# A recurrent segment loop on one core: output projection in four column quarters, the last tokens projected at the end

## The chip, the cores and the metric

The kernel runs on one core of one Trainium2 chip, with TensorE (matmul), VectorE, ScalarE, GpSimd, SyncE and the core's 16 DMA engines. The metric is the device time of one execution in microseconds, as a median of runs; a profiled execution of the same kernel gives the page and the trace that are read here.

## What is computed

Two independent parts write the two halves of the columns of one output, 2048 x 2048 in bf16. Part A is a long convolution (`_A_ref`), which the change leaves alone. Part B is a transformer layer with a memory that is passed from segment to segment:

```python
mem = mem0                                    # [1, 8, 1024]
for s in range(64):                           # 64 segments of 32 tokens
    h = concatenate([mem, x[:, 32*s:32*s+32]])          # 40 rows of 1024
    q, k, v = (einsum('btd,dhe->bhte', h, W) for W in (Wq, Wk, Wv))   # 32 heads of 128
    p = softmax(where(mask, einsum('bhqe,bhke->bhqk', q, k) * scale, -1e9))
    o = einsum('bhte,hed->btd', einsum('bhqk,bhke->bhqe', p, v), Wo)  # 40 rows of 1024
    mem = o[:, :8]                            # next segment's memory
    outs.append(o[:, 8:])                     # this segment's 32 tokens
```

The memory rows of one segment's output are input rows of the next, so the segments run one after the other.

## The kernel before

Part A runs first, with the parts of B that need no memory beside it: K, Q and V of the last 8 tokens of every segment, which are stored in the DRAM tensors RKQ (K and Q) and VBD (V). Then the loop over 64 segments runs from an order written out by hand (`tc.manual_schedule`): every engine executes its instructions in the order of the source, and semaphores make it wait. Each segment handles 32 rows on TensorE, 8 of memory and the first 24 tokens; the last 8 tokens join as keys, values and queries from RKQ and VBD.

**Weights.** The four matrices are cut in 64 pieces of 512 KB (128 x 2048 bf16): 16 each of Wk, Wq and Wv by rows (`kc`) and column half (`g`), and 16 head pairs (`hp`) of Wo. Most stay in SBUF under the names Wres, Wmid, Wmore, Wlate, pw, Wring and whole. The positions in STREAM of the list ORDER are streamed instead: `fetch` (L736) loads them from a DRAM copy WS into a ring of five slots (`wring`), on SP's queue, and `done` (L911) frees a slot after a piece's last matmul and fetches the next. Two of the streamed pieces of Wo (KEPT_A, pair 13, and KEPT_B, pair 9) are read once and kept as four quarters each in unused columns of PSUM; from segment 1 on VectorE copies a quarter to SBUF (`quarter` L893, `quarter_b` L856, through `bits`, L851) before its matmuls. 13 pieces are left to load in each segment.

**A segment.** `Proj.run` (L980) multiplies the 32 rows by a piece of Wk, Wq or Wv in four groups of 32 columns of the array, 512 columns each, into a PSUM bank; `evac` (L993, L989) copies the bank to SBUF on ScalarE. `transposes` turns K and Q (L935, L1002), `scores` (L1008, L1011) multiplies them in PSUM, `softmax_a` and `softmax_b` (L1015, L1025) run on VectorE with one exponential on ScalarE, and `attend` (L1052, L1056) multiplies by V. All this happens for two halves of 16 heads (g = 0 and 1). In the scores' block of eight groups of 40 columns, groups 0 to 3 belong to the 32 rows, one for each of four heads, and groups 4 to 7 to the last 8 tokens, for which one of the four groups is the right one for a row (`rowhead`).

**The output projection.** `evac_o` (L1064) copies the attention output OT of 16 heads to SBUF, 40 columns a head. `project` (L1074) takes 64 of these columns as weights (24 are of the next head and not used) and multiplies one head by 256 columns of Wo, in two groups of 64 columns of the array (`dh`), which hold the two halves of the 1024 output columns; `f` chooses 256 of the 512 in a half, in PSUM bank `yacc[f]`. So f = 0 and f = 1 are two passes. The order is: pairs 0 to 5, then `attend(1)`, pairs 6 and 7 while OT1 leaves PSUM, then the heads of g = 1 with the kept quarters laid between them, at last the five pairs of LAST for f = 0 and for f = 1. Each `yacc[f]` goes to the SBUF tile Y (L1170), and `fill_mem` (L778) turns the memory rows of Y into the next segment's input hT by matmuls with an identity and a copy on VectorE (L780). Two DMAs on GpSimd's queue store 32 rows of 512 columns each (L1172).

**GpSimd's queue in a segment, in order:** `load_kq` of the next segment (L930) within the projection, the two output stores, `keys(0)` (L964, a copy that needs `load_kq`), two VBD loads (L959), `keys(1)`, and `load_x` of the next segment (L769), which waits until V's matmuls have read the one buffer `rec`.

**SBUF rooms.** A tile `arena` of 21 blocks of 128 columns holds the segment's small data; `room(name, n)` is n blocks from a named start: C 0, D 4, B 8, KT1 12, A 13, KQ 17.

Of the kernel before, what the change touches and what calls it, by code (L numbers as in the profile page):

```python
# [9 lines left out]
BF = mybir.dt.bfloat16  # L10
# [11 lines left out]
FIRST, LAST = (0, 1, 2, 3), (10, 15, 11, 12, 14)  # L22
KEPT_A, KEPT_B = (3, 13, 0), (3, 9, 0)
WHOLE = (3, 4, 0)
O_ORDER = (*FIRST, 4, 5, 6, 7, 9, 13, 8, *LAST)
ORDER = [(0, kc, 0) for kc in (0, 1, 4, 5)] + [(1, kc, 0) for kc in (0, 1)] + [(0, kc, 0) for kc in (2, 3, 6, 7)] + \
    [(1, kc, 0) for kc in range(2, 8)] + [(m, kc, 1) for m in (0, 1) for kc in range(8)] + \
# [407 lines left out]
def b_kernel(ctx: ExitStack, tc, x, mem0, Wq, Wk, Wv, Wo, outb, n_seg, run_a):  # L435
    nc = tc.nc
# [41 lines left out]
    RKQ = dram.tile([n_seg // 16, 4, 128, 16, 128], BF, name="RKQ")  # L478
    VBD = dram.tile([2, n_seg, 8, 16, 128], BF, name="VBD")
# [41 lines left out]
    def stage1_done(su, vl, spare):  # L521
        make_consts()
        pools["mid"] = ctx.enter_context(tc.tile_pool(name="b_wmid", bufs=1, reuse_waits="tile"))
        for i, ch in enumerate(parts[0]):
            res[ch] = pools["mid"].tile([128, 2048], BF, name=f"Wmid{i}")[:]
# [246 lines left out]
    mem_cols = ident[:].rearrange("p (dh x) -> p dh x", dh=2)[:, :, 0:NM]  # L772

    def fill_mem(hT, Y, half, wide=32, tp=None):
        tp = tps[:, 0, 0:128].bitcast(F32) if tp is None else tp
        for j in (2 * half, 2 * half + 1):
            for e in range(0, 128, wide):
                nc.tensor.matmul(tp[e:e + wide, 16 * j:16 * j + 16], lhsT=Y[:, j * 128 + e:j * 128 + e + wide], rhs=mem_cols,  # L778
                                 start=True, stop=True, skip_group_check=True, tile_position=(0, e))
        nc.vector.tensor_copy(  # L780
            hT.rearrange("p (dh j) t -> p dh j t", dh=2)[:, :, 2 * half:2 * half + 2, 0:NM],
            tp.rearrange("p (j dh r) -> p dh j r", j=4, dh=2)[:, :, 2 * half:2 * half + 2, :])

    with c0p:
# [17 lines left out]
        Y = room("D", 4)  # L802
        nc.vector.memset(Y, 0.0)
        with tc.issue_after(got[-1].ins):
            load_x(0)
            for dh in range(2):
                nc.gpsimd.dma_start(Y[64 * dh:64 * dh + NM, :], mem0[:, dh * 512:(dh + 1) * 512])
        for g in range(2):
# [3 lines left out]
            for tb in range(4):  # L812
                if g == 1 and tb == 3:
                    for half in range(2):
                        fill_mem(pend[0], Y, half, tp=ps0.tile([128, 64], F32, tag="ps0", name="mem_ps")[:])
# [40 lines left out]
    def quarter_b(q, tag):  # L856
        t = room(tag, 4).bitcast(I32)
        w = []
        for home, at in B_homes[q]:
            n = home.shape[1] * (home.shape[2] if len(home.shape) == 3 else 1)  # L860
            bits(like(t[:, at:at + n], home), home)
            part = room(tag, 4)[:, 2 * at:2 * at + 2 * n]
            for dh, o in enumerate(quarter_cols(q)):
                lo, hi = max(at, 128 * dh), min(at + n, 128 * dh + 128)
                if lo < hi:
                    w.append((o + 2 * lo - 256 * dh, o + 2 * hi - 256 * dh, part[:, 2 * (lo - at):2 * (hi - at)]))
        return w

    def quarter_cols(q):
        return [1024 * (q // 2) + 512 * dh + 256 * (q % 2) for dh in range(2)]  # L870

    def keep(ch):
        t = live[0, ch][1]
        if kept[ch] == "A":
            w = t[:].bitcast(I32).rearrange("p (hh dh f x) -> p hh f dh x", hh=2, dh=2, f=2)
            for q in range(4):
                bits(OTi[:, q, 160:416].rearrange("p (dh x) -> p dh x", dh=2), w[:, q // 2, q % 2])
        else:
            w = t[:].bitcast(I32)
            for q in range(4):  # L880
                for home, at in B_homes[q]:
                    n = home.shape[1] * (home.shape[2] if len(home.shape) == 3 else 1)
                    if len(home.shape) == 3 and n > 128:
                        for dh, o in enumerate(quarter_cols(q)):
                            bits(home[:, 2 * dh:2 * dh + 2, :], w[:, o // 2:o // 2 + 128].rearrange("p (b x) -> p b x", b=2))
                        continue
                    for dh, o in enumerate(quarter_cols(q)):
                        lo, hi = max(at, 128 * dh), min(at + n, 128 * dh + 128)
                        if lo < hi:
                            src = w[:, o // 2 + lo - 128 * dh:o // 2 + hi - 128 * dh]  # L890
                            bits(home if len(home.shape) == 3 else home[:, lo - at:hi - at], like(src, home))

    def quarter(q, tag):  # L893
        t = room(tag, 4)
        bits(t.bitcast(I32), OTi[:, q, 160:416])
        return [(o, o + 256, t[:, 256 * dh:256 * dh + 256]) for dh, o in enumerate(quarter_cols(q))]
# [41 lines left out]
    with tc.manual_schedule():  # L938
# [6 lines left out]

        def seed_scores():
# [5 lines left out]
        for s in range(n_seg):  # L952
# [62 lines left out]
            def softmax_a(tag):  # L1015
                mx = one.tile([128, 8], F32, tag="mx", name="mx")
                nc.vector.tensor_reduce(out=mx[:], in_=S, op=ALU.max, axis=AX.X)  # L1017
                E = room(tag, 5).bitcast(F32).rearrange("p (b k) -> p b k", b=8)
                nc.vector.tensor_tensor(out=E, in0=S, in1=mx[:].unsqueeze(2).to_broadcast([128, 8, 40]),  # L1019
                                        op=ALU.subtract)  # L1020
                seed_scores()
                nc.scalar.activation(E, E, ACT.Exp, scale=scale)  # L1022
                return E

            def softmax_b(E, tag):  # L1025
                ssum = one.tile([128, 8], F32, tag="mx", name="ssum")
                nc.vector.tensor_reduce(out=ssum[:], in_=E, op=ALU.add, axis=AX.X)
                nc.vector.reciprocal(ssum[:], ssum[:])
                nc.vector.tensor_tensor(out=ssum[:, 4:8], in0=ssum[:, 4:8], in1=rowhead[:], op=ALU.mult)
                nc.vector.tensor_tensor(out=P_pad[:, 0:4, 0:32], in0=E[:, 0:4, 0:32],  # L1030
                                        in1=ssum[:, 0:4].unsqueeze(2).to_broadcast([128, 4, 32]), op=ALU.mult)
                own = P_pad[:].rearrange("p b k -> p (b k)")[:, 32:320].rearrange("p (i w) -> p i w", w=72)
                nc.vector.tensor_tensor(out=own[:, 0:4, 0:8], in0=E[:, 0:4, 32:40],
                                        in1=ssum[:, 0:4].unsqueeze(2).to_broadcast([128, 4, 8]), op=ALU.mult)
                nc.vector.tensor_tensor(out=E[:, 4:8, :], in0=E[:, 4:8, :],
                                        in1=ssum[:, 4:8].unsqueeze(2).to_broadcast([128, 4, 40]), op=ALU.mult)
                nc.vector.tensor_copy(P_pad[:, 4, 32:64].rearrange("p (i t) -> p i t", i=4), E[:, 4:8, 32:40])
                with nc.allow_low_precision("one of the four terms is not zero"):
                    nc.vector.tensor_reduce(out=P_pad[:, 4, 0:32], in_=E[:, 4:8, 0:32].rearrange("p i k -> p k i"),
                                            op=ALU.add, axis=AX.X)  # L1040
                PT = room(tag, 3)[:, 0:320].rearrange("p (kb i q) -> p kb i q", kb=2, i=4)
                for kb in range(2):
                    ks = slice(32 * kb, 32 * kb + 32)
                    nc.vector.transpose(out=PT[:, kb, :, 0:32], in_=P_pad[:, 0:4, ks])
                    nc.vector.transpose(out=PT[:, kb, :, 32:40], in_=P_pad[:, 4, ks])
                return PT

            def attend(g, PT, V):
                for i in range(4):
                    w = V[i // 2][:, i % 2 * 128:i % 2 * 128 + 128]  # L1050
                    for c in range(4):
                        nc.tensor.matmul(OTp[:, c, i * 40:i * 40 + 40], lhsT=w[32 * c:32 * c + 32, :],  # L1052
                                         rhs=PT[32 * c:32 * c + 32, 0, i, :], start=(i == 0), stop=False,
                                         tile_position=(32 * c, 0), skip_group_check=True)
                for c in range(4):
                    nc.tensor.matmul(OTp[:, c, 0:160], lhsT=VBs[g][32 * c:32 * c + 32, :],  # L1056
                                     rhs=PT[32 * c:32 * c + 32, 1].rearrange("p i q -> p (i q)"), start=False, stop=True,
# [4 lines left out]
            def evac_o(g):  # L1062
                OT = room("B" if g else "C", 5).rearrange("p (c i q) -> p c i q", c=4, i=4)
                nc.scalar.copy(OT, o_view)  # L1064
                return OT

            def project(h, f, w, OT, stop=False):
                k = 40 * (h % 16)
                m = min(64, 640 - k)
                lhsT = OT.rearrange("p c i q -> p (c i q)")[:, k:k + m]  # L1070
                for dh in range(2):
                    o = (h % 2) * 1024 + dh * 512 + f * 256
                    for x, y, r in columns(w, o, o + 256):
# [171 lines left out]
```

## Time and profile before

| what | time or size |
|---|---|
| runs | 1716.27, 1721.94, 1723.39 us (median 1721.94) |
| profiled execution, own time | 1717.88 us |
| its span on the core | 1716.0 us |
| part A and setup, to the first output projection | 398 us |
| TensorE busy | 1644.0 us (96%) |
| VectorE, ScalarE, GpSimd busy | 1033.6, 675.9, 348.8 us |
| moved by DMA | 598.03 MB, mean 348 GB/s |
| TensorE clock granted in the loop | full |

A page has the busy time of each engine, the span in 40 slices, the DMA queues, the chain of work that ended last, and the costliest groups of instructions. Matmuls are pipelined: a single one lasts 379 ns, but a new one can start long before, so the rate is read from how many matmuls fill a stretch, not from the length of one.

### The profile page before, as it was taken

Reading aid. Unit: us, or ns where it says so; the run is one execution under the profiler, and the core shown is the slowest. Engines: PE = TensorE matmul, PEld = TensorE weight load, DVE = VectorE, ACT = ScalarE, POOL = GpSimd, SP = SyncE. Lnnn points to the kernel's source line nnn. Section 1 sums busy time; section 2 is a strip of 40 time slices with the busy share of each in tenths; the row PEclk is TensorE's granted clock in tenths of the full one; section 3 lists DMA queues with packets and bytes.
Section 4 is the critical chain, followed back from the end, with each engine's and each line's share of the span. In section 5 each row is a group of like instructions: output and inputs, shape, how many; then the busy total and the mean of one; then the engine's idle time right before and its main releaser. Section 6 shows DMA issues by size and latency. Waiting matters only on the chain. (4 is left out here: it accounts for less than half of the span.)

```text
span 1716.0 us, 71162 instructions
## 1 busy us (share of the span) xinstructions
PE 1644.0 (96%) x30776; PEld 996.9 (58%) x30776; DVE 1033.6 (60%) x3463; ACT 675.9 (39%) x1250; POOL 348.8 (20%) x626
## 2 busy tenths in 40 slices
PE   6899988998999999999999999999999999999998
PEld 3443333445666666666666666666666666666665
DVE  9968853235555555656666555555565656655555
ACT  6876741103333333333333333333333333333333
POOL 4113431101122111211211212121121112111121
PEclk9999998999999999999999999999999999999999
DMA  9989999989999999999999999999999999999997
GB/s 330 391 310 378 373 346 372 357 321 374 344 346 341 346 350 348 360 342 353 352 353 354 341 354 344 340 357 352 347 350 347 352 333 355 356 345 342 349 354 277
DMA packets 180830, 598.03 MB, mean 348 GB/s; under 512 B 24658, under 2 KB 24674, under 8 KB 180516
## 3 DMA queue, kind: packets, MB, share of 16 engines
q1 hardware_dynamic: 151860, 525.80, 84.4%
q0 software_dynamic: 19984, 44.61, 7.4%
q10 hardware_dynamic: 8672, 23.07, 3.4%
q8 instruction: 241, 3.95, 0.9%
q14 instruction: 73, 0.60, 0.1%
HBM read 538.33 MB, written 57.15 MB: 347 GB/s over the span
## 5 line engine op out<-in xcount | busy, mean ns | idle before, releaser
L980 PEld LDWEIGHTS <-rec 128*32 128x32 bf16 x12288 | 298.4, 96 | 284.0 <-DVE rec L780 36.3
L1074 PEld LDWEIGHTS <-arena 128*64 128x64 bf16 x8255 | 430.0, 109 | 51.6 <-ACT arena L1064 33.4
L993 ACT CAST arena<-acc 128x512 bf16<-128x512 f32 x320 | 187.0, 584 | 359.7 <-PE acc L980 288.0
L980 PE MATMUL acc<-Wres,rec 128*32 128x512 bf16 x3328 | 251.0, 381 | 3.2 <-issue 3.2
L980 PE MATMUL acc<-wring,rec 128*32 128x512 bf16 x2300 | 227.5, 380 | 4.4 <-issue 1.6
L980 PE MATMUL acc<-Wmid,rec 128*32 128x512 bf16 x3072 | 211.7, 379 | 0.3 <-issue 0.2
L1074 PE MATMUL yacc<-Wmore,arena 128*64 128x256 bf16 (+1 forms) x2560 | 207.6, 273 | 0.2 <-issue 0.2
L1064 ACT CAST arena<-OTp 128x640 bf16<-128x640 f32 x128 | 88.6, 692 | 197.6 <-PE OTp L1056 177.0
L1104 DVE COPY arena<-OTp 128x512 bf16<-128x512 bf16 x64 | 27.2, 425 | 230.3 <-PE OTp L935 230.3
L1074 PE MATMUL yacc<-wring,arena 128*64 128x256 bf16 x2064 | 159.8, 274 | 3.5 <-DMA wring<-WS 1.8
L851 DVE TENSOR_SCALAR arena<-OTp 128x256 int32<-128x256 int32 x378 | 128.0, 394 | 38.0 <-ACT arena L1064 35.2
L1074 PE MATMUL yacc<-arena 128*64 128x256 bf16 x1071 | 141.1, 270 | 0.1
L1170 ACT CAST arena<-yacc 128x256 bf16<-128x256 f32 x128 | 47.7, 373 | 230.2 <-PE yacc L1074 226.7
L980 PE MATMUL acc<-pw,rec 128*32 128x512 bf16 x1796 | 121.8, 379 | 2.1 <-issue 1.4
L959 POOL DMA_DIRECT2D arena<-VBD x128 | 68.3, 534 | 259.7 <-DVE arena L1019 104.6
L980 PE MATMUL acc<-Wlate,rec 128*32 128x512 bf16 x1536 | 117.0, 381 | 0.0
L780 DVE CAST rec<-tps 128x32 bf16<-128x32 f32 x126 | 24.2, 192 | 148.8 <-PE tps L778 148.8
L1172 POOL DMA_DIRECT2D out_dram<-arena x128 | 65.8, 514 | 203.7 <-ACT arena L1170 200.4
L930 POOL DMA_DIRECT2D arena<-RKQ x64 | 49.6, 775 | 253.5 <-PE yacc L1074 244.4
L1017 DVE TENSOR_REDUCE mx<-SB 128x8 f32<-128x320 f32 x128 | 62.7, 490 | 47.0 <-PE SB L1011 43.6
L1022 ACT ACTIVATE arena<-arena 128x320 f32<-128x320 f32 x128 | 60.3, 471 | 69.0 <-DVE arena L1019 60.5
L769 POOL DMA_DIRECT2D rec<-REC x64 | 35.9, 561 | 247.9 <-PE acc L980 244.2
(225 smaller groups left out, 2633.5 us busy)
## 6 DMA issues: line engine op xcount, KB each, us to landing
wring<-WS SPq DMA_DIRECT2D x831, 512.0 KB, 5.9
SK<-s_sb SPq DMA_DIRECT2D x16, 512.0 KB, 7.6
SU<-s_sb SPq DMA_DIRECT2D x16, 512.0 KB, 6.7
Kg<-SK SPq DMA_DIRECT2D x32, 256.0 KB, 5.8
Ug<-SU SPq DMA_DIRECT2D x32, 256.0 KB, 5.5
RKQ<-stage ACTq DMA_DIRECT2D x16, 512.0 KB, 9.6
zt<-SZ SPq DMA_DIRECT2D x16, 512.0 KB, 10.6
arena<-RKQ POOLq DMA_DIRECT2D x64, 128.0 KB, 5.7
```

The lines of the kernel that those rows point to most:

```text
L769: nc.gpsimd.dma_start(rec[:], REC[:, s, :])
L851: nc.vector.tensor_scalar(out=dst, in0=src, scalar1=0, scalar2=None, op0=ALU.bitwise_or)
L930: nc.gpsimd.dma_start(rec.rearrange("p (j c) -> p j c", j=4), RKQ[s // 16, :, :, s % 16, :].rearrange("j p c -> p j c"))
L959: nc.gpsimd.dma_start(VB, VBD[g, s].rearrange("t h e -> h t e"))
L980: nc.tensor.matmul(self.acc[32 * c:32 * c + 32, :], lhsT=hT[:, ch[1], :], rhs=w[:, 512 * c:512 * c + 512], start=(ch == chs[0]), stop=(ch ...
L993: nc.scalar.copy(sb, self.acc[:])
L1017: nc.vector.tensor_reduce(out=mx[:], in_=S, op=ALU.max, axis=AX.X)
L1022: nc.scalar.activation(E, E, ACT.Exp, scale=scale)
L1064: nc.scalar.copy(OT, o_view)
L1074: nc.tensor.matmul(yacc[f][64 * dh:64 * dh + m, x - o:y - o], lhsT=lhsT, rhs=r, start=(h == (0, 2 * FIRST[-1])[f] and x == o), stop=stop, ...
L1170: nc.scalar.copy(Y[:, 256 * f:256 * f + 256], yacc[f][:, 0:256])
L1172: nc.gpsimd.dma_start(bass.AP(outb.tensor, outb.offset + SEG * s * 2048 + 512 * dh, [[2048, 32], [1, 512]]), Y[64 * dh + NM:64 * dh + 40, :])
```

## The change

- Each head's projection takes exactly its 32 columns of OT as weights, in four groups of 32 columns of the array at once, each for a quarter of the 1024 output columns (`head_out`). One PSUM bank `Yb` holds all 256 columns of the four quarters, so pairs 0 to 9 need one pass of 256 columns, and LAST two passes of 128.
- The last 8 tokens of each segment are no longer projected in the loop. `evac_last` copies their columns of OT and stores them on GpSimd's queue in a DRAM tensor OLD (two stores of 32 KB a segment, rows of 256 bytes). After the loop they are loaded in four blocks of 16 segments (`last_rows`), put in order by head (`by_heads`) and multiplied as 128 rows by all of Wo; the six streamed pieces of Wo are loaded again for it (`ends`).
- Output in the loop is 24 rows in four stores of 256 columns.
- The right group of scores for the last 8 tokens is selected (a multiply and a sum) ahead of the softmax, which then works on five groups instead of eight; two transposes replace four.
- All eight pairs of g = 0 (EARLY) come ahead of `attend(1)`. Kept quarters come in another order, two of them (B0 and A2) copied on ScalarE; `load_kq` follows quarter A2.
- PSUM banks of the projections alternate with the segment's parity; the copy of Q after its first transposition moves to ScalarE; the order of `kc` within K and Q changes with the layout of the memory rows. The streamed positions stay the same.

```diff
+EARLY, LAST = (0, 1, 2, 3, 4, 5, 6, 7), (10, 15, 11, 12, 14)
+O_ORDER = (*EARLY, 9, 13, 8, *LAST)
+ORDER = [(0, kc, 0) for kc in (0, 2, 4, 6)] + [(1, kc, 0) for kc in (0, 2)] + [(0, kc, 0) for kc in (1, 3, 5, 7)] + \
+    [(1, kc, 0) for kc in (4, 6, 1, 3, 5, 7)] + [(m, kc, 1) for m in (0, 1) for kc in range(8)] + \
...
+        def last_rows(b):
+            for g in range(2):
+                raw[b, g] = home(6 + 2 * b + g, "OLr")
+                nc.sync.dma_start(raw[b, g][:].rearrange("p (s w) -> p s w", s=16), OLD[:, g, 16 * b:16 * b + 16, :])
+        def by_heads(b, engines):
+            for g in range(2):
+                OLs[b, g] = home(2 * b + g if b < 3 else 14 + g, "OL")
+                engines[g](
+                    OLs[b, g][:].rearrange("p (h s t) -> p h s t", h=16, s=16),
+                    raw[b, g][:].rearrange("p (s h t) -> p h s t", s=16, h=16))
...
-                    self.acc = bank(g if m == 2 else m, "acc")
+                    self.acc = bank((g if m == 2 else m) ^ s % 2, "acc")
...
+                nc.vector.tensor_tensor(out=own, in0=S[:, 4:8, :], in1=rowhead[:].unsqueeze(2).to_broadcast([128, 4, 40]),
+                                        op=ALU.mult)
+                nc.vector.tensor_reduce(out=S[:, 4, :], in_=own.rearrange("p i k -> p k i"), op=ALU.add, axis=AX.X)
+                nc.vector.tensor_reduce(out=mx, in_=S[:, 0:5, :], op=ALU.max, axis=AX.X)
...
-                nc.scalar.copy(OT, o_view)
+                main = OT[:, 0:512].rearrange("p (c i q) -> p c i q", c=4, i=4)
+                for c in range(0, 4, 2 if g else 4):
+                    cs = slice(c, c + (2 if g else 4))
+                    nc.scalar.copy(main[:, cs], o_view[:, cs, :, 0:32])
+            def evac_last(g, OT):
+                nc.scalar.copy(OT[:, 512:640].rearrange("p (c i q) -> p c i q", c=4, i=4), o_view[:, :, :, 32:40])
+                nc.gpsimd.dma_start(OLD[:, g, s, :], OT[:, 512:640])
+            def head_out(h, lo, hi, OT, rhs_of, stop=False):
+                for qd in range(4):
+                    nc.tensor.matmul(Yb[32 * qd:32 * qd + 32, lo:hi], lhsT=OT[:, 32 * (h % 16):32 * (h % 16) + 32],
+                                     rhs=rhs_of(qd), start=(h == 0), stop=stop, skip_group_check=True,
+                                     tile_position=(0, 32 * qd))
...
             V1 = pv1.evac()
+            evac_last(0, OT0)
+            if last:
+                for b in range(3):
+                    last_rows(b)
+                for i, hp in enumerate(hp for hp in O_ORDER if (3, hp, 0) in streamed):
+                    ends[hp] = home(16 + i, "Wend")[:]
+                    nc.sync.dma_start(dst_view(ends[hp], (3, hp, 0)), dram_chunk((3, hp, 0)))
+                by_heads(0, [nc.gpsimd.tensor_copy] * 2)
+            Yb = bank(s % 2, "yacc")
+            for hp in EARLY:
+                out_cols(hp, 0, 256, OT0)
+            qs = {}
+            if s:
+                qs["B", 0] = quarter_b(0, "KQ", by_act)
             attend(1, PT1, (V1[:, 0:256], V1[:, 256:512]))
             OT1 = evac_o(1)
+            if s:
+                qs["A", 0], qs["B", 2] = quarter(0, "C", bits), quarter_b(2, "A", bits)
+                out_quarter(KEPT_B, 0, qs["B", 0])
+                qs["A", 2] = quarter(2, "KQ", by_act)
+                steps = {(0, 0): [("A", 0), ("B", 1, "C", bits)], (0, 2): [("B", 2), ("B", 3, "A", bits)], (0, 3): [("A", 2)],
+                         (1, 1): [("B", 1), ("A", 1, "C", bits)], (1, 2): [("B", 3), ("A", 3, "A", bits)],
+                         (1, 4): [("A", 1), ("A", 3)]}
...
+            evac_last(1, OT1)
+            out_cols(8, 0, 256, OT1)
...
+                            if step == ("A", 2) and not last:
+                                load_kq(s + 1)
...
+            for q in range(4):
+                nc.gpsimd.dma_start(bass.AP(outb.tensor, outb.offset + SEG * s * 2048 + 256 * q, [[2048, NX], [1, 256]]),
+                                    Y[32 * q + NM:32 * q + 32, :])
+            if last:
+                last_rows(3)
+        for b in range(4):
+            if b < 3:
+                by_heads(b + 1, [nc.vector.tensor_copy, nc.scalar.copy])
             for dh in range(2):
+                z = bank(dh, "z")
+                for h in range(32):
+                    o = 1024 * (h % 2) + 512 * dh
+                    nc.tensor.matmul(z[:], lhsT=OLs[b, h // 16][:, 128 * (h % 16):128 * (h % 16) + 128],
+                                     rhs=ends.get(h // 2, res.get((3, h // 2, 0)))[:, o:o + 512], start=h == 0, stop=h == 31)
+                zs = room("C" if dh else "B", 4)
+                (nc.vector.tensor_copy if dh else nc.scalar.copy)(zs, z[:])
+                nc.sync.dma_start(bass.AP(outb.tensor, outb.offset + (512 * b + NX) * 2048 + 512 * dh,
+                                          [[SEG * 2048, 16], [2048, 8], [1, 512]]), zs)
```

`out_cols(hp, lo, hi, ...)` calls `head_out` for the two heads of a pair, and `out_quarter` for one kept quarter.

More of the change, by code (lines that the diff above doesn't have):

```diff
@@ L1062, in evac_o @@
             def evac_o(g):
-                OT = room("B" if g else "C", 5).rearrange("p (c i q) -> p c i q", c=4, i=4)
-                nc.scalar.copy(OT, o_view)
-                return OT
[L1067 to L1073, printed above, removed]
-                        nc.tensor.matmul(yacc[f][64 * dh:64 * dh + m, x - o:y - o], lhsT=lhsT,
-                                         rhs=r, start=(h == (0, 2 * FIRST[-1])[f] and x == o), stop=stop,
-                                         tile_position=(0, 64 * dh))
```

210 lines of the change are left out of this document (88 added, 122 removed).

## The prediction

> **What bounds the kernel now.** I read the page's slices and queues first, then the chain of waits for one segment, then the timeline of the same stretch of another, then windows for the transfers.
>
> ```profile
> PE   6899988998999999999999999999999999999998
> DMA  9989999989999999999999999999999999999997
> q1 hardware_dynamic: 151860, 525.80, 84.4%
> wring<-WS SPq DMA_DIRECT2D x831, 512.0 KB, 5.9
> ```
>
> TensorE and the 16 DMA engines are both full from the tenth slice on. Nearly all that moves is the weight ring (`wring`): 13 pieces of 512 KB in each of the 64 segments.
>
> ```profile
> 1332.19 2.74 PE yacc L1074 x48
> 1334.93 0.20 PE OTp L1052 x16
> 1335.13 0.07 PE OTp L1056 x4
> 1335.21 4.14 PE yacc L1074 x72
> 1339.35 0.06 PE tps L778 x2
> 1339.41 0.46 PE yacc L1074 x8
> 1339.87 0.98 PE acc L980 x16
> 1340.85 0.04 PE tps L778 x7
> 1340.88 3.32 PE acc L980 x60
> 1344.20 0.45 PE OTp L935 x32
> ...
> 1352.31 2.74 PE yacc L1074 x48
> ```
>
> In the chain, one segment is TensorE alone and takes 20.12 us from one output projection to the next: 7.68 us of projection (1332.19 to 1339.87), then 12.44 us of K, Q, V and attention. From 1270.14 to 1703.87 the same row comes 21 times later, so the mean segment is 433.73/21 = 20.65 us; the 0.53 us over 20.12 are scattered gaps. From the start of the first projection (398.36 in the timeline) to that of the last (1703.80) lie 63 segments, and 12.2 us from there to the end.
>
> ```profile
> 285.00:305.00 20.00, 17.30 (x85) 8.02 (x84) 8.26 (x9) 3.52 (x6) 1.99 (x3) 0.91 1.03 419
> 1001.00:1006.00 5.00, 5.00 (x106) 4.42 (x103) 3.94 (x18) 1.43 (x3) 0.56 (x1) 1.00 1.00 371
> 1006.00:1011.00 5.00, 5.00 (x104) 3.64 (x104) 1.84 (x8) 0.75 (x2) 1.80 (x3) 1.00 0.93 317
> 1011.00:1016.00 5.00, 5.00 (x140) 2.69 (x132) 1.72 (x4) 1.76 (x3) 1.04 (x3) 1.00 1.01 364
> ```
>
> The last two columns are the DMA engines' share and GB/s. Within the loop a share of 1.00 goes with about 370 GB/s: of the forty 5 us windows from 500 to 700 us, the 17 with a share of 1.00 or more have a mean of 372 and reach from 347 to 390. From 500 to 1700 us the mean is 349 GB/s, so a segment moves 349 x 20.65 = 7.21 MB. The DMA engines are thus hardly looser than TensorE, though TensorE rarely waits for `wring` by name: the five ring slots are refilled 5.9 us ahead.
>
> **What the change removes on TensorE.** Rates come from the chain. Four 32-column groups at 512 columns: 3.32/15 = 0.221 us for four (L980). At 128 columns: 0.45/8 = 0.056 us for four (L935). Two 64-column groups at 256 columns: 0.114 us for two (L1074). Four at 256 columns appear nowhere; half of 0.221 and the whole of 0.114 bound them at 0.110 and 0.114, and I take 0.112. After: heads of EARLY 16 x 0.112 = 1.8; pair 8, 0.22; eight quarters of kept weights, 0.45; LAST, 20 x 0.056 = 1.1. That is 3.6 us of matmul where 7.4 stood.
>
> **What gives most of it back.** The old matmuls were cover. Let S be the start of the projection.
>
> ```profile
> 1019.46 0.49 DVE L1017 TENSOR_REDUCE mx<-SB 128x8 f32<-128x320 f32 x1
> 1021.31 0.49 DVE L1027 TENSOR_REDUCE ssum<-arena 128x8 f32<-128x320 f32 x1
> 1023.70 0.17 DVE L1045 STREAM_TRANSPOSE arena<-P_pad 128x32 bf16<-128x32 bf16 x1
> 1023.98 0.17 PEld L1052 LDWEIGHTS <-arena 32*128 32x128 bf16 x16 [0.20 <-issue]
> ```
>
> Here S = 1021.24. The second softmax starts on VectorE at S-1.78 and lets `attend(1)` go at S+2.74. The new one puts a multiply (L1035's size, 0.34) and a reduction (L1039's, 0.37) ahead; maximum and subtraction shrink from 0.49 to about 0.37 (320 elements to 200). With the 0.14 us between dependent operations the sum starts at S+0.85 instead of S+0.07. Behind it, fewer operations take 2.1 us for 2.6. So `attend(1)` goes at about S+3.05, while EARLY is done at S+1.8: 1.25 us idle. Then 0.28 for `attend(1)`; then OT1 must leave PSUM (two ScalarE halves of L989's 0.375, plus 0.3 of semaphores) before any OT1 head can start: 0.65 idle, which pairs 6 and 7 used to cover. From S+4.0 there are 1.8 us of matmuls, laid between kept quarters copied out of PSUM at 0.36 to 0.59 us each into three rooms in turn; I count waits of 0.1 (A2), 0.3 (B3), 0.35 (A3) and 0.15 for `fill_mem`. Sum: S+6.7, against S+7.68. The other side of the same step: `load_x` issues at S+0.49 and lands 5.2 later in the middle (4.3 to 6.5), and the next K needs it and a 0.19 copy, so S+6.1 is the floor and S+7.4 the bad case. I take 6.7. Bank alternation and QT0 on ScalarE get nothing: TensorE is busy in `k1.run(5)` while QT0 is copied, and the next K starts with no wait for the accumulators' banks in the chain above. TensorE's segment: 12.44 + 6.7 + 0.53 = 19.65 us.
>
> **The transfers.** Ring loads stay 13. Added per segment: two stores of 32 KB into OLD; output falls from 64 to 48 KB. 7.21 + 0.05 = 7.26 MB, at 372 GB/s 19.5 us; bounds 18.6 (390) and 20.9 (347). Two limits at 19.65 and 19.5 with gaps that don't fall together: I add 0.25 and take 19.9, a gain of 0.75 us a segment, 63 x 0.75 = 47 us.
>
> By the Trainium skill (DMA: Bandwidth & Descriptors, Specifications) a core gets about 358 GB/s from HBM; that would be 20.3 us a segment and a time some 25 us longer than mine. The trace disagrees: 419 over 20 us above, in another mix of transfers.
>
> **What it adds at the end.** 4 blocks x 2 banks x 32 full matmuls of 512 columns, which L820 shows at 0.216 (three in 0.81, one in 0.38): 55.3 us, with nothing beside them to hide under. Before them: the last ring load is issued at S-1.6 and lands 5.9 later, S+4.3; behind it on SP's queue come six OLD loads and six Wo pieces, 1.35 us each at about 385 GB/s. The two halves of OLD's block 0 are there at S+5.7 and S+7.0, and two GpSimd copies of 2048 elements take 1.9 (a memset of 2176 takes 2.0) to 4.6 us each (four times 1.155 of L368); 3 puts the first matmul at S+8.8. The first bank stalls for Wo pieces: pair 8 is eleventh in the queue, S+19.1, and 16 heads follow: S+22.6. Seven more banks at 6.9: S+71. Copy, store and landing 3.5: S+74.5, against S+12.2. Cost 62 us; 55 if no Wo piece is late, 67 at the slow copy.
>
> **Sum.** 1716.0 + 62 - 47 = 1731 us. The profiled execution's span is 5.9 under the median of the runs shown (1721.94), so 1737. Changes under 0.5% (8.6 us) can't be told from none.
>
> **Rivals.**
> - The transfers keep up. With slots freed sooner the ring asks earlier; windows of 385 to 390 GB/s exist, and the end's loads ran at 419 elsewhere. Then 18.6 for the DMA, TensorE near 19.2 as ring waits swallow its gaps: gain 1.45 x 63 = 91, end 59: 1684, as a run 1690. Against it: those are single windows between ones at 355 to 375.
> - The two limits overlap wholly: 19.65, gain 1.0, 63 against 62: 1721, no change.
> - GpSimd's small transfers come late, slower than before. `load_kq` moves behind quarter A2 and behind the second OLD store: issue at about S+5.8 (before S+4.8), landing 5.7 later, `keys` 0.3, the VBD load 5.3: 10.6 us into the next QKV, where `attend(0)` wants it at 10.97. 0.3 us of slack against landings of 4.0 to 7.5. With 0.6 us lost a segment (20.5) the gain is 0.15: 1769, as a run 1775. It decides once the landings are 0.4 over their medians together. The OLD stores belong here: 256 rows of 256 B; at q0's 78 ns a packet (4.9% of 16 x 1200 us over 12064) over 16 engines nothing to 1.25 us, and I took nothing, as RKQ's 256 B rows show no price; at the far end 1790. The Trainium skill (same page, Specifications) says that below 512 B the DMA reads, modifies and writes; no store of this trace has such rows, and it is one reason for this rival's chance.
>
> **How the numbers follow.** Forecast 0.42 (1728 to 1750 by itself), transfers keep up 0.25, no change 0.15, late small transfers 0.18. Slower by over 0.5%: 0.18 + 0.36 = 0.54. Within: 0.10 + 0.06 = 0.16. Faster: 0.25 + 0.05 = 0.30. The range leaves out the far halves of the outer cases: 1695 to 1778.
>
> **What would show it.** Projection of 6.7 us in the chain, with idle TensorE ahead of `attend(1)` (about 1.2) and ahead of the first OT1 head (0.65); DMA share 1.00 and 365 to 375 GB/s in all windows; segments near 19.9; some 70 us of L820-like matmuls at the end, their first bank stretched to 13 us. Wrong if windows run at 385 and more, if segments are under 19.5, or if `attend(0)` waits for VBD in most segments.

## The result and the profile after

| | before | after |
|---|---|---|
| median of the runs shown together | 1722.66 us | 1908.41 us (1899.62 to 1916.87, 4 runs) |
| ratio, 95% interval | | 1.1085 (1.1028 to 1.1143) |
| span of the profiled execution | 1716.0 us | 1915.1 us |
| mean of 62 segments (from the second projection on) | 20.67 us | 22.74 us |
| least segment | 20.12 us | 20.40 us |
| start of the last projection to the end | 12.2 us | 79.6 us |

The kernel is 11% slower; 1737 us was forecast. The two spans differ by 199 us: 63 segments at 2.07 us more are 130, the end is 67 more, and the rest lies ahead of the loop. So the loop, which was to gain 47 us, lost 130.

The page of the changed kernel first (slices of the span, DMA queues, groups of instructions with their idle time, DMA issues):

```profile
PE   6998979978888888888888878888888888988879
PEclk9999999989999999999998888899998889899989
DMA  9999999899999998899999988999999889999870
...
q1 hardware_dynamic: 155796, 534.19, 78.1%
...
q8 instruction: 268, 4.39, 0.9%
...
L988 PEld LDWEIGHTS <-rec 128*32 128x32 bf16 x12288 | 327.5, 101 | 313.8 <-issue 76.6
...
L1083 PEld LDWEIGHTS <-arena 128*32 128x32 bf16 x11760 | 257.1, 102 | 222.3 <-issue 151.8
...
wring<-WS SPq DMA_DIRECT2D x831, 512.0 KB, 5.5
```

In the kernel before, the weight loads of the projection read:

```profile
L1074 PEld LDWEIGHTS <-arena 128*64 128x64 bf16 x8255 | 430.0, 109 | 51.6 <-ACT arena L1064 33.4
```

TensorE has fallen from 9 to 8 in most slices, but the DMA engines have not become the bound in its place: their share falls too. Two things are new. The granted clock drops to 8 tenths in places, where it was full throughout the loop. And over 150 us of waiting ahead of the weight loads of the projection carry the name "issue": nothing that the profile shows ends them. The timeline of TensorE in one projection shows both kinds of wait, named and not:

```profile
1128.72 0.50 PE L1083 MATMUL yacc<-Wlate,arena 128*32 128x256 bf16 x12
...
1131.35 0.28 PE L1059 MATMUL OTp<-arena 32*128 32x40 bf16 x16 [0.81 <-DVE arena L1052]
...
1132.22 0.24 PE L1083 MATMUL yacc<-arena 128*32 128x128 bf16 x4 [0.52 <-ACT arena L1074]
...
1132.95 0.24 PE L1083 MATMUL yacc<-arena 128*32 128x128 bf16 x4 [0.16 <-DVE arena L849]
...
1133.98 0.24 PE L1083 MATMUL yacc<-arena 128*32 128x128 bf16 x4 [0.34 <-ACT arena L952]
...
1134.69 0.30 PE L1083 MATMUL yacc<-wring,arena 128*32 128x128 bf16 x8 [0.36 <-ACT arena L1185]
...
1135.39 0.23 PE L1083 MATMUL yacc<-Wring,arena 128*32 128x128 bf16 x1
1137.80 0.29 PE L1083 MATMUL yacc<-Wring,arena 128*32 128x128 bf16 x7 [2.18 <-issue]
...
1138.10 0.43 PE L988 MATMUL acc<-wring,rec 128*32 128x512 bf16 x4
```

Five waits have a releaser and return in most segments (each in 48 to 60 of 60). The sixth, 2.18 us, falls in the middle of one head pair, between the first and the second of eight matmuls that need the same data. No semaphore stands there. What does stand there is a block border of TensorE's instructions: queue q8 moves them in 268 packets of 16384 bytes, and its 4.39 MB over TensorE's 68,264 instructions (34,113 matmuls and 34,151 weight loads) are 64 bytes each, so one packet brings a block of 256. The packets in the trace beside the standstills named issue and over 0.6 us long, from 1120 to 1240 us:

```
q8 packet (us)       TensorE stands still   first instruction after the packet's end
1135.36 - 1136.36    1135.62 - 1137.80      1.44
1159.79 - 1160.74    1159.86 - 1162.05      1.31
1183.44 - 1184.48    1184.90 - 1185.85      1.37
1208.23 - 1209.32    1209.87 - 1210.63      1.31
1232.36 - 1233.42    1234.20 - 1234.91      1.49
```

From 450 to 1650 us, 34 of the 36 standstills named issue and over 0.8 us long end 1.2 to 1.6 us after such a packet. The five in the table lie four blocks apart, which is 1024 of TensorE's records (its sequencer's included), and a segment has 1008; so each comes 16 records later in its segment than the one before, here out of the projection into K (the last two).

Numbering all these records shows that the standstills lie on block borders: from 430 to 1700 us there are 59 standstills of over 0.3 us named issue, and the first record behind each has a number that leaves 161 when divided by 256. The packets pair with the blocks one to one throughout. TensorE had run out of instructions.

### The profile page after: what moved, and what is told of

The parts are those of the page before. It is cut to its first block, busy times and chain, and to the rows that moved or that the text cites. A ratio compares the mean times of both kernels' runs of the same rounds, so it can differ in the third digit from the quotient of the medians.

```text
span 1915.1 us, 78411 instructions
## 1 busy us (share of the span) xinstructions
PE 1632.2 (85%) x34113; PEld 875.3 (46%) x34151; DVE 958.3 (50%) x3031; ACT 770.2 (40%) x1639; POOL 486.4 (25%) x886
## 3 DMA queue, kind: packets, MB, share of 16 engines
q8 instruction: 268, 4.39, 0.9%
## 4 chain that ended last, share of the span: by engine, by line
PE 56%; DVE 19%; ACT 9%; issue 9%; DMA 6%; ACTq 0%; POOL 0%; SPq 0%; DVEq 0%; POOLq 0%
PE acc L988 26%; PE yacc L1083 9%; PE kb_ps L640 4%; PE z L1199 3%; PE vb_ps L818 2%; DVE arena L849 2%; ACT arena L1112 2%; PE OTp L921 2%; PE OTp L1010 2%; DVE SB L1028 2%; ACT arena L952 2%; DMA zt<-SZ 1%; DVE arena L1110 1%; DVE arena L1029 1%; DVE arena L1030 1%
## 5 line engine op out<-in xcount | busy, mean ns | idle before, releaser
L1083 PEld LDWEIGHTS <-arena 128*32 128x32 bf16 x11760 | 257.1, 102 | 222.3 <-issue 151.8
L1083 PE MATMUL yacc<-arena 128*32 128x128 bf16 x2016 | 130.7, 248 | 76.7 <-ACT arena L1074 32.6
L1083 PE MATMUL yacc<-Wmore,arena 128*32 128x128 bf16 (+1 forms) x3584 | 154.9, 256 | 22.2 <-issue 22.0
L1187 POOL DMA_DIRECT2D out_dram<-arena x256 | 130.5, 514 | 108.1 <-ACT arena L1185 104.4
L988 PE MATMUL acc<-Wlate,rec 128*32 128x512 bf16 x1536 | 155.2, 462 | 3.0 <-issue 3.0
L1083 PE MATMUL yacc<-wring,arena 128*32 128x256 bf16 (+1 forms) x2576 | 120.7, 263 | 29.3 <-ACT arena L1185 23.6
L1079 POOL DMA_DIRECT2D OLD<-arena x128 | 70.0, 547 | 279.4 <-issue 269.3
L1074 ACT CAST arena<-OTp 128x256 bf16<-128x256 f32 (+1 forms) x192 | 78.9, 445 | 136.2 <-PE OTp L1063 105.7
L1026 DVE TENSOR_TENSOR arena<-SB,rowhead 128x160 f32<-128x160 f32 x128 | 41.6, 325 | 120.5 <-PE SB L1019 78.8
L1033 ACT ACTIVATE arena<-arena 128x200 f32<-128x200 f32 x128 | 47.5, 371 | 130.9 <-PE acc L988 72.2
```

The lines of the kernel that those rows point to most:

```text
L988: nc.tensor.matmul(self.acc[32 * c:32 * c + 32, :], lhsT=hT[:, ch[1], :], rhs=w[:, 512 * c:512 * c + 512], start=(ch == chs[0]), stop=(ch ...
L1026: nc.vector.tensor_tensor(out=own, in0=S[:, 4:8, :], in1=rowhead[:].unsqueeze(2).to_broadcast([128, 4, 40]), op=ALU.mult)
L1033: nc.scalar.activation(e, e, ACT.Exp, scale=scale)
L1074: nc.scalar.copy(main[:, cs], o_view[:, cs, :, 0:32])
L1079: nc.gpsimd.dma_start(OLD[:, g, s, :], OT[:, 512:640])
L1083: nc.tensor.matmul(Yb[32 * qd:32 * qd + 32, lo:hi], lhsT=OT[:, 32 * (h % 16):32 * (h % 16) + 32], rhs=rhs_of(qd), start=(h == 0), stop=sto ...
```

## The experiments

Three theories were set against each other: that the named waits are the whole loss; that they let the clock fall, and half clock is the loss; and that instructions come late, because a block of 256 is fetched through the same DMA engines that the weight ring keeps full.

**Full clock without the change's waits.** `after_fill` gives TensorE idle work in its four longest waits, two of them shown:

```diff
+            def busy(n):
+                for _ in range(n if s > 1 else 0):
+                    nc.tensor.matmul(spare[:], lhsT=ident[:], rhs=res[WHOLE][:, 0:512], start=True, stop=True, ...)
...
+            busy(4)
             attend(1, PT1, (V1[:, 0:256], V1[:, 256:512]))
             OT1 = evac_o(1)
+            busy(3)
```

> Changed kernel with 11 matmuls of 128x512 a segment, each about 0.216 us, that write an unused PSUM bank while TensorE waits anyway: four ahead of attend(1), three ahead of the first OT1 head, two ahead of quarter A2, two between the passes of LAST. Theory clock (a 3.41 us window in which TensorE is under about 60% busy is followed by one at half clock): the 218 us of half clock in the loop fall under 70 us, a segment gets about 1.2 us shorter, the time falls by 60 to 95 us to 1815 to 1850. Theory waits alone (the time went into the waits themselves): no gain, 1905 to 1925. Theory instruction supply: the 50 or so stalls of 0.6 to 3 us named issue stay, since nothing is taken from the instructions; it is at most one part of the loss.

Measured: 1902.78 us (1.1058, 1.0992 to 1.1123). In the window from 1450 to 1650 us (busy time and count of TensorE's matmuls and weight loads, VectorE, ScalarE, GpSimd, then granted clock, DMA share, GB/s) the changed kernel has

```profile
1450.00:1650.00 200.00, 169.77 (x4330) 99.43 (x4330) 91.64 (x326) 75.50 (x178) 53.78 (x105) 0.89 0.89 313
```

and with the fillers

```profile
1450.00:1650.00 200.00, 184.50 (x4515) 98.72 (x4511) 97.33 (x347) 79.56 (x187) 52.00 (x102) 0.99 0.91 317
```

The clock is back, half clock in the loop fell from 218 us to 34, and the time moved by 6 us. The fillers have a price of their own: the least segment grew by 0.31 us (20.40 to 20.71), some 19 us in all. Even with these added, the gain stays far under the 60 to 95 us of the clock theory, which falls as an account of the loss. The standstills named issue stayed: 1.27 us a segment from 450 to 1650 us without the fillers, 1.20 with them.

**Waits alone, in the kernel before.** `before_idle2` and `before_idle4` move `attend(1)` ahead of pairs 4 and 5, or 2 to 5, so that it waits for the softmax:

```diff
-            out_proj((4, 5), OT0)
             attend(1, PT1, (V1[:, 0:256], V1[:, 256:512]))
...
-                out_proj((6, 7), OT0)
+                out_proj((4, 5, 6, 7), OT0)
```

> Kernel before with attend(1) moved ahead of pairs 4 and 5: TensorE then waits about 0.9 us in each segment for the second softmax, and nothing else changes. Both theories: 63 x 0.91 = 57 us more, 1780 (1765 to 1795), granted clock 1.00 in the loop, since a 3.41 us window with 0.9 us of waiting is still 73% busy.

> Kernel before with attend(1) moved ahead of pairs 2 to 5: a wait of about 1.8 us in each segment. Theory waits alone: 63 x 1.83 = 115 us more, 1838 (1820 to 1850), clock full. Theory clock: in some 70% of the segments a window holds more than 1.37 us of the wait, so half clock follows for 3.41 us at 1.7 us each: 75 us on top, 1913 (1880 to 1945), granted clock under 0.97.

Measured: 1750.94 us (1.0190, 1.0147 to 1.0232) and 1809.18 us (1.0522, 1.0476 to 1.0569). Segments grew by 0.57 and 1.43 us, less than expected, because the softmax of the kernel before is done at S+2.38, not at S+2.74: there TensorE had come last. 63 times these are 36 and 90 us, and the runs show 32 and 91. Half clock came once in `before_idle4` (3.4 us): waits of this size cost their own length here and no more. As a test of the clock the run is weak, since only two of its stretches of 3.41 us fell under 60% busy.

**More instructions for the same work.** `before_split` cuts most projection matmuls of the kernel before in two:

```diff
-                    for x, y, r in columns(w, o, o + 256):
+                    halves = [c for i in (0, 128) for c in columns(w, o + i, o + i + 128)] if s and ... else columns(w, o, o + 256)
+                    for x, y, r in halves:
```

> Kernel before with most projection matmuls of 256 columns cut in two of 128: the same columns in all, 238 more TensorE instructions a segment (538 in the projection for 300). Theory instruction supply (instructions come in blocks of 256, one block ahead, and a fetch takes 3.4 to 7.5 us): a block lasts 3.7 us in the projection, stalls named issue of 0.5 to 2 us appear about once a segment, 1750 to 1830. Theory that only waits and clock count: 1722 to 1730, no such stalls.

Measured: 1884.18 us (1.0964, 1.0888 to 1.1040), more than expected. Nothing waits that did not wait before, and yet the groups of its page read as those of the changed kernel do:

```profile
L1075 PEld LDWEIGHTS <-arena 128*64 128x64 bf16 (+1 forms) x15752 | 481.4, 111 | 155.5 <-issue 122.3 <-ACT arena L1064 24.0 <-ACT arena L1022 1.5
```

59 of its 61 standstills named issue and over 0.8 us long end 1.2 to 1.6 us after an instruction packet, and all 103 of over 0.3 us from 430 to 1700 us lie on one grid of 256 records.

**Fewer transfers for the same instructions.** `after_half`, `after_fill_half`, `before_half` and `before_split_half` load 7 ring pieces a segment instead of 13. They leave out six loads and multiply by a piece that lies in SBUF in their place, so their output is not the layer's:

```diff
+    unloaded = [ch for ch in order_s if ch not in kept][1::2]
...
+        if now[0] > 1 and ch in unloaded:
+            return [(0, 2048, res[WHOLE])]
```

> Changed kernel that loads 7 instead of 13 ring pieces a segment from segment 2 on; the six others are replaced by a piece that lies in SBUF (the result is then another one, the instructions of TensorE are the same). Theory instruction supply through the DMA engines (a block of 256 instructions is fetched only when the block before it has begun, and the fetch queues behind the ring's transfers): the fetches come sooner, the stalls named issue go, a segment falls from 22.7 us towards the 20.4 of its best ones, 1765 to 1825 by what half clock stays. Rival, a limit of TensorE's own or of the named waits: no change, 1890 to 1920. Rival, half clock bounds: since the waits stay, at most the 0.97 us of stalls go and the clock stays, 1840 to 1860.

> The same with the filling matmuls of the first run of this study, so that the clock stays full. Supply theory: segments at 20.7 to 20.9 us, 1785 to 1805; with the run without fillers it gives what the clock costs once the instructions arrive. Rival (a limit that does not hang on transfers): 1885 to 1910.

> Kernel before with the same six loads left out. Supply theory: its scattered gaps (0.53 us a segment over the least of 20.12) are late instructions and shrink to 0.1 or 0.2: 1690 to 1705. Rival (they are something else, or the transfers bound nothing): 1715 to 1725.

> The kernel before with split matmuls (238 more instructions a segment, 1884 us in its run) and with six ring loads a segment left out. Supply theory: the same instructions then arrive in time, segments 20.2 to 20.6 us, 1690 to 1715. Rival (matmuls of 128 columns are slow in themselves): 1830 and more.

Measured: 1794.96 (1.0440, 1.0398 to 1.0482), 1789.11 (1.0398, 1.0368 to 1.0429), 1685.72 (0.9801, 0.9767 to 0.9836) and 1719.94 us (1.0004, 0.9985 to 1.0022). The first two lie in their expected ranges, the third 4 us under its range and the fourth 5 us over. The same window of `after_half`:

```profile
1450.00:1650.00 200.00, 176.07 (x4892) 99.58 (x4896) 105.73 (x378) 86.36 (x203) 60.18 (x118) 1.00 0.62 201
```

With a DMA share of 0.62 the standstills named issue are gone (0.01 us a segment for 1.27), while the named waits are as long as before; the middle half of the segments take 20.40 to 20.54 us. The kernel before, which seemed bound by TensorE, gains as well: its segments fall from 20.67 to 20.16. And the split matmuls, 166 us dear with all loads, cost 34 without them, 9 of it (20.27 for 20.13 us) in the best segments. So it is the pairing of many instructions with busy DMA engines that costs; TensorE waits for `wring` in none of these runs worth naming.

The pairing of packets and blocks shows what the loads change. From 450 to 1650 us:

| kernel | DMA share | packet starts after the block before it has begun, median (nine in ten under), us | packet, median, us | standstills named issue, us a segment |
|---|---|---|---|---|
| before | 0.97 | 2.72 (3.56) | 1.02 | 0.21 |
| before_split | 0.90 | 2.60 (3.72) | 1.03 | 2.21 |
| before_split_half | 0.61 | 1.24 (2.27) | 0.97 | 0.16 |
| after | 0.91 | 2.40 (3.97) | 1.00 | 1.27 |
| after_half | 0.61 | 1.21 (2.24) | 0.97 | 0.01 |

A packet takes about as long in all of them; with fewer loads it starts 1.2 to 1.4 us sooner. What holds it back in the DMA engines is not seen in the traces; that it queues behind the ring's transfers stays an argument.

**Fewer instructions for the same work.** `after_onepass` (over `after_fill`) runs LAST once with 256 columns, with six more fillers:

```diff
+                for n, hp in enumerate(LAST):
+                    out_cols(hp, 0, 256, OT1, n == 4)
...
+                nc.scalar.copy(Y[:, 0:256], Yb[:, 0:256])
+                if not last:
+                    fill_mem(pend[s + 1], Y, 0, 64)
```

> The changed kernel with fillers, where LAST runs once with 256 columns instead of twice with 128 from segment 1 on: about 66 TensorE instructions a segment fewer, the same columns; the wait for the copy to Y between the passes (0.5 us) goes, but at the end the next K waits some 1.3 us for Y and fill_mem. Supply theory: fewer blocks count more than the longer tail, segments 21.4 to 22.0 us, 1835 to 1875. Theory waits alone: about 0.8 us a segment longer than with fillers, 1950.

`before_fewer` and `after_fewer` turn the first K and Q in eight full transposes and run `fill_mem` 128 wide; `before_tr` keeps only the transposes:

```diff
-            turned_k, turned_q = transposes(k0, 0, True), transposes(q0, 128, True)
+            turned_k, turned_q = transposes(k0, 0), transposes(q0, 128)
...
-                fill_mem(hT, Y, 1)
+                fill_mem(hT, Y, 1, 128)
```

> Kernel before with the first transposes of K and Q as eight matmuls of 128 columns instead of 32 in groups, and fill_mem in four instead of twelve: 64 TensorE instructions a segment fewer (842 for 906), the same work. Supply theory: of the 0.52 us a segment that went when fewer transfers were loaded, more than half goes, 1690 to 1705. Rival (instructions are not late in the kernel before, or full transposes are dearer by as much): 1715 to 1730.

> The changed kernel with the same edit: 56 instructions a segment fewer (948 for 1004), 0.22 of a block of 256. Supply theory at the 5.8 us a block that the changed kernel takes: 1.1 to 1.4 us a segment less, 1820 to 1845. Rivals (named waits or half clock bound the loop): 1895 to 1915.

> Kernel before with only the transposes of K and Q as eight full matmuls (48 instructions a segment fewer; fill_mem as it was, since its wide form cost 0.44 us a segment in the run with 64 fewer). Supply theory: the least segment grows by 0.11 us (the stretch from the first transposition to the scores took 1.64 for 1.53 there), the late instructions fall from 0.53 to some 0.2: 1700 to 1712, faster than both kernels. Rival (the 0.53 came from elsewhere): 1722 to 1730.

Measured: 1908.11 (1.1096, 1.1059 to 1.1132), 1727.43 (1.0054, 1.0037 to 1.0070), 1910.39 (1.1110, 1.1073 to 1.1148) and 1711.46 us (0.9956, 0.9941 to 0.9972). Three of four expectations missed, and `before_fewer` and `after_fewer` came out where their rivals had put them. So the least and the mean segment have to be read apart; their difference is taken here as the time lost to late instructions and half clock (`after_onepass` from the third projection on, where its fillers begin):

| kernel | TensorE instructions a segment | ring loads | least, us | mean, us | mean less least |
|---|---|---|---|---|---|
| before | 906 | 13 | 20.12 | 20.67 | 0.55 |
| before_half | 906 | 7 | 20.13 | 20.16 | 0.03 |
| before_fewer | 842 | 13 | 20.67 | 20.82 | 0.15 |
| before_tr | 858 | 13 | 20.34 | 20.60 | 0.26 |
| before_split_half | 1144 | 7 | 20.27 | 20.71 | 0.44 |
| after | 1004 | 13 | 20.40 | 22.74 | 2.34 |
| after_fill | 1026 | 13 | 20.71 | 22.52 | 1.81 |
| after_fewer | 948 | 13 | 20.63 | 22.75 | 2.12 |
| after_onepass | 958 | 13 | 22.06 | 22.59 | 0.53 |
| after_fill_half | 1026 | 7 | 20.71 | 20.80 | 0.09 |

In `before_fewer` the lateness did go (0.55 to 0.15), but the wide forms made the work itself 0.55 us longer. `before_tr` keeps the better part, at the upper edge of its range: 0.4% under the kernel before, it is the only run here that beats both kernels with all the work done. `after_fewer` shows that the sum of instructions doesn't decide: 56 fewer, most of them outside the projection, left the difference at 2.12. In `after_onepass`, 68 fewer in the projection itself, it fell from 1.81 to 0.53, but the longer tail (1.35 us more in the least segment, where 0.8 was reckoned) gave it all back. That tail is also time in which instructions can arrive, so the run doesn't show which of the two brought the difference down.

The fetch runs about one block ahead: as the table of packets shows, a block's packet starts only around or after the time at which the block before it begins, so a block with slack lends none to the next. How long TensorE took for a block matters, but does not decide by itself. In the changed kernel, from 430 to 1700 us, 28 of the 56 blocks that took under 5.0 us (the standstill itself not counted) ended in one of over 0.3 us, 30 of the 120 that took 5.0 to 6.1 us, and 1 of the 43 that took longer. In the kernel before it was 17 of the 144 under 6.1 us, and none of the 74 over.

**Two parts put at nothing.** `before_bankqt` alternates the projections' banks and copies the turned Q on ScalarE in the kernel before; `after_half_qt` takes the copy back to VectorE in `after_half`:

```diff
-            nc.vector.tensor_copy(QT0, turned_q)
+            nc.scalar.copy(QT0, turned_q)
```

> Kernel before with two parts of the change that the prediction put at nothing: the projections' banks alternate, and Q's copy after its first transposition is on ScalarE. The prediction's own account: 1718 to 1724. Account from the best segments of the changed kernel (0.30 us longer from the first transposition to the first scores, because the copy on ScalarE starts only when the one on VectorE is done): up to 19 us more, 1730 to 1740.

> The changed kernel with six ring loads a segment left out and Q's copy after its first transposition on VectorE again. If that copy costs 0.30 us a segment, as its best segments show: 1795 - 19 = 1776 (1770 to 1782), and 1.53 us from the first transposition to the scores. If it costs nothing, as the prediction had it: 1795.

Measured: 1763.34 (1.0265, 1.0231 to 1.0300) and 1781.14 us, 14 less than `after_half`. The timeline of the changed kernel shows what the copy does:

```profile
1306.11 0.42 DVE L1110 COPY arena<-OTp 128x512 bf16<-128x512 bf16 x1 [5.21 <-PE OTp L921]
1306.62 0.59 ACT L1112 COPY arena<-OTp 128x512 bf16<-128x512 bf16 x1 [1.03 <-DVE arena L1110]
...
1307.26 0.28 PE L1016 MATMUL SB<-arena 128*32 128x40 bf16 x16
```

In the kernel before, both copies are on VectorE:

```profile
1344.71 0.42 DVE L1104 COPY arena<-OTp 128x512 bf16<-128x512 bf16 x1 [3.55 <-PE OTp L935]
1345.05 0.41 DVE L1106 COPY arena<-OTp 128x512 bf16<-128x512 bf16 x1
...
1345.56 0.27 PE L1008 MATMUL SB<-arena 128*32 128x40 bf16 x16
```

The two copies read one PSUM tile, and the second starts when the first is done: 1.15 us from the first copy to the scores, where two copies in a row on VectorE took 0.85. From the first transposition to the scores it is 1.83 for 1.53 us, and 1.53 again in `after_half_qt`. The other part of `before_bankqt` says nothing of the change: there a projection fills both banks, and with alternation every second segment waits 0.69 us for V's bank and 0.46 for Y's, which the changed kernel, with one bank for the projection, doesn't do.

## Why the prediction was wrong

**Instructions, the step that failed.** The working counted columns ("four at 256 columns", "20 x 0.056") and bytes ("7.26 MB, at 372 GB/s 19.5 us"), and no step asked how many instructions these columns come in. The projection has 206 matmuls for 153, each with its weight load, in less time, and over the whole loop two thirds of the standstills named issue fall in it (0.81 of 1.21 us a segment). "Scattered gaps" of 0.53 us were carried over from the kernel before as if they were fixed; `before_half` shows that nearly all of them go when fewer ring pieces are loaded, so they were mostly late instructions already. Half clock, which nothing in the forecast held, is the smaller part: it costs 0.33 us a segment where instructions come in time (`after_half`, 20.40 to 20.73 from the third segment on), and with the fillers, which take most of it away, the mean less the least fell by 0.53 (2.34 to 1.81). How the 2.34 divide exactly stays open.

**The account by terms.** Forecast 19.9 us a segment, measured 22.74. (12.44 + 6.7 + 0.53 make 19.67, not the 19.65 of the working; with 0.25 they are 19.92.)

| term | forecast | measured | difference |
|---|---|---|---|
| projection, least undisturbed | 6.7 | 7.57 | +0.87 |
| K, Q, V and attention, least | 12.44 | 12.83 | +0.39 |
| scattered gaps and overlap of limits (0.53 + 0.25); late instructions, half clock | 0.78 | 2.34 | +1.56 |

63 x 2.82 is 178 us, and the end 5 more: 183 of the 184 us by which the span passed the 1731 of the sum.

**The projection's waits.** The matmul prices held: 0.109 us for four of 256 columns (forecast 0.112) and 0.055 at 128 (0.056). The wait before `attend(1)` is 1.0 us by the start times, not 1.25 (the trace's own 0.82 counts from the recorded end of the last matmul): it goes at S+2.74, not S+3.05, because the old softmax, from which the forecast counted on, was done at S+2.38 (`before_idle2`), not at the S+2.74 at which the old `attend(1)` began. The wait for OT1 is 0.6 by the start times (0.65). What was missed stands behind it: 3.96 us from the first OT1 head to the next K where 2.7 was reckoned. A2's copy on ScalarE delays its head by 0.5 (forecast 0.1), A0's copy by 0.33, and the second pass of LAST waits 0.5 us for the copy of the first out of the same bank `Yb`, where the kernel before had a bank for each. These are readings of the trace; only Q's copy was undone by a run.

**"Bank alternation and QT0 on ScalarE get nothing."** True of the banks as far as the trace goes; false of the copy, 0.30 us a segment. The cover named (`k1.run(5)`) is 1.08 us long, and the copies outlast it once one waits for the other.

**The transfers.** A DMA share of 1.00 and 365 to 375 GB/s were named as the mark; it is 0.88 to 0.94 and 308 to 328 over stretches of 200 us. None of the rivals came: the ring is not faster, the limits do not cancel, and `attend(0)` doesn't wait for VBD. The DMA engines do decide, but by how late they deliver 16 KB of instructions, not by how many bytes they move. The Trainium skill (Runtime: NRT & Kernel Launch, Instruction fetch mechanics) describes blocks of 256 instructions that the sequencer fetches while it executes the present one, and calls the cost mostly hidden. The block size agrees with the 16384 bytes of q8, and so does the start of the packets; that the cost is hidden holds here at a DMA share of 0.62, and not at 0.9.

**The end.** Forecast S+74.5, measured S+79.6. The timeline of its first bank:

```profile
1845.87 0.61 PE L1199 MATMUL z<-Wlate,OL 128*128 128x512 bf16 x1
1846.70 1.06 PE L1199 MATMUL z<-Wlate,OL 128*128 128x512 bf16 x2 [0.22 <-issue]
...
1850.56 0.59 PE L1199 MATMUL z<-Wend,OL 128*128 128x512 bf16 x2 [1.98 <-DMA Wend<-in_B_Wo_dram]
...
1856.18 1.86 PE L1199 MATMUL z<-Wend,OL 128*128 128x512 bf16 x4 [2.25 <-DMA Wend<-in_B_Wo_dram]
...
1862.78 0.59 ACT L1202 CAST arena<-z 128x512 bf16<-128x512 f32 x1 [14.32 <-PE z L1199]
```

It starts at S+10.3 (forecast 8.8), stalls twice for pieces of Wo as foreseen, and ends at S+26.9 (22.6): most of the 32 matmuls go at 0.43 us, since the clock is at half from 1845 to 1862 but for 3.4 us. Seven more banks take 48.5 us, 6.93 each, for the 6.9 reckoned. The step was right but for the clock and a first bank that began 1.5 us later.

## What to carry to other kernels

Count instructions as well as columns. Cutting the work of a matmul into narrower groups keeps the instructions and shortens the time in which they must arrive; "issue" ahead of weight loads in the page is the sign that they came late. In the changed kernel, at a DMA share of 0.91, half of the blocks of 256 TensorE instructions that were used up in under 5.0 us ended in a standstill, and nearly none of those that took over 6.1 us. That agrees with the sum of the steps: the packet starts 2.40 us after the block before it has begun (in one case of ten 3.97 or more), takes 1.00, and no block from 450 to 1650 us began sooner than 1.16 us after its packet's end, which makes 4.6 to 6.1 us. A wait that TensorE's work covered comes back whole when that work shrinks, so list what each removed matmul hid; and before a lower clock is blamed for lost time, fill the idle engine and see whether the time follows, with the price of the filling counted.

## What the runs showed of the hardware

- From 450 to 1650 us no two instruction packets start less than 3.28 us apart in any of the sixteen traces, and the median packet takes 0.96 to 1.03 us; TensorE goes on 1.2 to 1.6 us after the end of the one it waits for. In the changed kernel each of the 59 standstills of over 0.3 us named issue lies on one grid of 256 records of TensorE.
- The granted clock fell to half in steps of 3.41 us without any long pause. In the loop of the changed kernel, of 56 stretches of 3.41 us at full clock in which TensorE was less than 60% busy, 40 were followed by one at half; of the 287 that were over 65% busy, none. The Trainium skill (TensorE: Matmul & The Clock Gate, Why this matters for your kernels) warns of pauses over some 3 us; the longest wait in each of these 40 stretches was 0.5 to 2.2 us, in 24 of them under 1 us. Yet in `after_half` only 11 of 33 stretches under 60% were followed by half clock, and in `before_split` 7 of 30, so the busy share of one stretch is not the whole rule.
- Matmuls over the full width of the array between groups of 32 columns cost time of their own: full transposes made the stretches before and after them 0.10 and 0.11 us longer for the same columns (`before_tr`), and `fill_mem` in its wide form added 0.33 more (`before_fewer`, 20.67 for 20.34 us).
